# Two 64 x 64 inverses at the start of an RWKV-7 kernel, taken from VectorE and DRAM to powers on TensorE

## The chip, the cores and the metric

The kernel runs on one core of one Trainium2 chip. The metric is the device time of one execution in microseconds. Before the change it is 537.99 us, the median of three runs (537.51 to 538.75).

## What is computed

The reference has two parts. The first is a recurrence over 768 tokens, for 4 batches and 8 heads of 40 elements each:

```python
for t in range(S):
    y[:, :, t] = einsum('bhd,bhde->bhe', r_t, state)
    Sa = einsum('bhde,bhe->bhd', state, a_t)
    state = state * w_t[:, :, None, :] - einsum('bhd,bhe->bhde', Sa, b_t) + einsum('bhd,bhe->bhde', v_t, k_t)
```

The second takes y as 3072 rows of 320 numbers and applies `h = x @ w_in` (320 x 1024), `solu = h * softmax(h)`, a layer norm with the gain `g_ln`, and `@ w_out` (1024 x 320). The weights come as 64-bit floating point numbers and are turned into fp32 on the chip.

## The kernel before, in words

**Chunks.** The recurrence is computed by chunks of 64 tokens (C = 64). A chunk i holds two batches p and all eight heads, so there are N = 24 chunks: chunks 0 and 1 are the first 64 tokens of all four batches, chunks 2 and 3 the next 64, and so on. Inside a chunk the tokens depend on each other through a strictly triangular 64 x 64 matrix per batch and head (16 of them in a chunk), made from the scaled keys b and a; what is needed is the inverse of the identity minus that matrix, which `solved` applies to the right-hand sides x0.

**How an inverse is made.** `norm(i)` multiplies bT and aT of chunk i on TensorE (16 products of 64 x 64), keeps the negative in `nt` and writes its two 32 x 32 diagonal blocks to DRAM (`nt_dram`). `invert(n)` serves two chunks (2n and 2n+1, GRP = 2): it reads the blocks back so that each of 64 blocks lies in a partition of its own (`blk`), and VectorE solves for the inverse column by column in some 30 steps of two to four small instructions (lines 508, 516 and 519). The result goes to DRAM (`uu_dram`). `bring(i)` loads it for chunk i into `tu` and `uh`, `flip(i)` transposes blocks on VectorE, and `couple(i)` and `close(i)` add the off-diagonal block by two sets of 16 products on TensorE with two ScalarE copies.

**How the weights come in.** Thirteen parts of weights (five of w_in with 512 columns, eight of w_out with 320) are loaded by `land(n, queue)` and turned into fp32 by `split`: `begin_narrow` ("b", two VectorE instructions), `scale_narrow` ("s", three ScalarE instructions), `end_narrow` ("f", three VectorE instructions, and for some parts the next load on GpSimd's queue).

**Order.** All engines run in the order in which the code issues. A prologue prepares chunks 0 to 3 (`decay`, `decay_turned`, `front`, `front_b`, `norm`), then a loop runs over i from -1 to 26. Pass i solves chunk i, prepares chunk i + 5, and multiplies chunk i - 2 by w_in (`hidden`) and chunk i - 3 by w_out (`output`). The dictionary `plans` puts VectorE's work on the weights and the inverses into each pass: in "b s 5" the letters are the steps of a split and a number is so many steps of the next inverse ("o1": only of an inverse that is already due). `vector(plan)` issues one such string.

**PSUM.** Each of the tags A, B, C and h is a pair of banks for one use at a time; `pair(tag, name)` takes it, and its next user waits until it has been copied out.

In the listing, `turned` makes eight transposes for one operand, `tokens` takes an SBUF tile of [128, 2, 4, 64], `half(p)` is one half of the partitions, `in_turn` orders products so that neighbours use different quarters of the array, and `mm` (line 285) is one product.

Of the kernel before, what the change touches and what calls it, by code (L numbers as in the profile page):

```python
# [33 lines left out]
def shape_constants():  # L34
    s, t = np.arange(P)[:, None], np.arange(P)[None, :]
    same = s // C == t // C
    row = np.arange(P)[:, None] % C
    parts = dict(
        ident=np.eye(P),
        cum=same & (s <= t),  # L40
        tri=row < np.arange(C)[None, :],
        eye_hi=row == Q + np.arange(Q)[None, :],
        hi=(row >= Q).astype(np.float64),
        mean=np.full((P, P), 2.0 ** -10),
    )
    at, where = 0, {}
    for name, x in parts.items():
        where[name] = (at, at + x.shape[1])
        at += x.shape[1]
    return np.concatenate([np.asarray(x, np.float64) for x in parts.values()], 1).astype(np.float32), where  # L50
# [3 lines left out]
def kernel(  # L54
# [90 lines left out]
    def pair(tag, name):  # L145
        return psum.tile([P, 2, 512], FP32, tag=tag, name=name)
# [85 lines left out]
    def vector(plan):  # L232

        for word in plan.split():
            if word in "bsf":
                dict(b=begin_narrow, s=scale_narrow, f=end_narrow)[word]()
            else:
                some(int(word.strip("o")), (i + 2) // GRP if "o" in word else N)
# [75 lines left out]
    def ok(i):  # L314
        return 0 <= i < N


    def load_keys(i, names, queue=nc.sync):
        if not ok(i):
            return  # L320
        for n, ap in (("w", w), ("b", b), ("a", a), ("k", k)):
            if n in names:
                x = a_t[i % 3] if n == "a" else two.tile([P, H, D], FP32, tag="raw_" + n, name="raw_" + n,
                                                             bufs=2 if n == "w" else 3)
                st[i]["raw_" + n] = x
                load(x, ap, i, queue)
# [59 lines left out]
    def scaled(i, names="bk"):  # L386
        if not ok(i):
            return
        d = st[i]
        kb = d["kb"] = kb_t[i % (AHEAD + 2)]  # L390
        for n in names:
            j = H * (n == "b")
            nc.gpsimd.tensor_tensor(out=kb[:, j:j + H, 0:D], in0=d["raw_" + n], in1=heads(d["inv"]), op=ALU.mult)  # L393
# [27 lines left out]
    def front(i, t=None, y=0):  # L421
        if not ok(i):
            return lambda: None
        d = st[i]
        t = turned(pair("C", "pa") if t is None else t, y, d["raw_a"])
        aT = d["aT"] = tokens("aT", AHEAD)
        return lambda: nc.vector.tensor_tensor(out=aT[0:W2], in0=t, in1=d["ex"][0:W2, :, :, 0:C], op=ALU.mult)
# [31 lines left out]
    def shared_pair(i):  # L459

        if i not in shared:
            shared[i] = pair(turn["Y"], "py")
        return shared[i]

    def norm(i):
        if not ok(i):
            return
        d = st[i]
        t = shared_pair(i - AHEAD + 1)
        for u in in_turn(lambda p, q, g, h: (h, p ^ h)):  # L470
            p, q, g, h = u
            at = 4 * Q + (2 * q + g) * C
            mm(t[half(p ^ h), p, at:at + C], keyed(d["bT"], u), keyed(d["aT"], u))
        nt = d["nt"] = tokens("nt", AHEAD)
        nc.scalar.mul(out=nt, in_=t[:, :, 4 * Q:4 * Q + 256].rearrange("p b (j c) -> p b j c", j=4), mul=-1.0)  # L475
        n, at = divmod(i, GRP)
        if at == 0:
            blocks[n] = dram.tile([2, 2 * GRP * H, Q, Q], FP32, tag="nt_dram", name="nt_dram")
        for x in range(2):
            for e in range(2):  # L480
                home = C * x + Q * e
                queue = nc.sync if 1 < i < 4 or i == 1 and x else nc.gpsimd
                queue.dma_start(out=blocks[n][e].rearrange("(a x h) s c -> a x s h c", a=GRP, x=2)[at, x],  # L483
                                  in_=nt[home:home + Q].rearrange("p h j c -> p (h j) c")[:, :, Q * e:Q * e + Q])

    def spread(n):
        nb = two.tile([P, Q, Q], FP32, tag="blk", name="blk")
# [37 lines left out]


    def bring(i):
        if not ok(i):  # L530
            return
        d = st[i]
        d["tu"], d["uh"] = tu_t[i % 2], uh_t[i % 2]
        n, at = divmod(i, GRP)
        src = inverse[n].rearrange("c (e a x h) t -> e a c x h t", e=2, a=GRP, x=2)
        for x in range(2):
            queue = nc.sync if i or not x else nc.gpsimd
            queue.dma_start(out=d["tu"][C * x:C * x + Q, :, Q:2 * Q], in_=src[0, at, :, x])
        for x in range(2):
            nc.sync.dma_start(out=d["uh"][C * x + Q:C * x + C], in_=src[1, at].rearrange("c x h t -> c (x h) t"))  # L540

    def flip(i):
        if not ok(i):
            return
        tu = st[i]["tu"]
        nc.vector.transpose(out=tu[:, :, 0:Q], in_=tu[:, :, Q:2 * Q])

    def couple(i):
        if not ok(i):
            return lambda: None  # L550
        d = st[i]
        t = shared_pair(i)
        for u in in_turn(lambda p, q, g, h: (p ^ h, p)):
            p, q, g, h = u
            j = 2 * q + g
            x = half(p ^ h)
            mm(t[half(p), h, j * Q:j * Q + Q], d["nt"][x, p, j], d["tu"][x, 4 * p + j, 0:Q])
        return lambda: nc.scalar.activation(out=wy[:, :, :, 0:Q], in_=t[:, :, 0:4 * Q].rearrange("p h (j c) -> p h j c", j=4),  # L558
                             func=AF.Copy, scale=c_("hi"))

    def close(i):
        if not ok(i):
            return
        d = st[i]
        t = shared_pair(i)
        for u in in_turn(lambda p, q, g, h: (p, p ^ h)):
            p, q, g, h = u
            j = 2 * q + g
            mm(t[half(p ^ h), p, 384 + j * Q:384 + j * Q + Q], wy[half(p), h, j], d["uh"][half(p), H * (p ^ h) + 4 * p + j])
        nc.scalar.copy(out=d["tu"].rearrange("p (h j) c -> p h j c", h=2)[:, :, :, 2 * Q:],  # L570
                       in_=t[:, :, 384:].rearrange("p h (j c) -> p h j c", j=4))
# [307 lines left out]
    def begin_inverse(n):  # L879
        steps.append((n, invert(n)))  # L880
        next(steps[-1][1])
# [5 lines left out]
        load_keys(i, "a")  # L887
    nc.scalar.dma_start(out=g_rows, in_=moe_g_ln.rearrange("(c p) -> c p", p=P))
    load_keys(2, "w")
    for n in range(2):  # L890
        land(n, nc.sync)
    load_keys(2, "ba")
    decay(0)()
    logged(1)
    decay_turned(0)()
    plans = {
        -6: ("", "", "", "", ""),
        -5: ("b", "", "b", "", "s f"),
        -4: ("", "s", "f", "6", "2"),
        -3: ("", "", "", "", "14"),  # L900
        -2: ("", "10"),
        -1: ("b o1 s 3", "f 5", "8", "", "", "b 4"),
        0: ("", "s", "3 b", "s 2 f", "2 b 1 s", "f"),
        1: ("f b 5", "s", "8 b f", "", "s b f o1 2", "o1 3"),
        2: ("b s 5", "f s b s", "f b 5 s f 1", "b 1", "s", "f"),
        3: ("1 f", "", "11", "1 o2", "", "1"),
        4: ("4", "", "12", "", "", ""),
        5: ("7", "", "7", "2", "1", "o1"),
        24: ("o2 2", "", "", "o9", "o4", "", ""),
        25: ("1", "2", "2", "8", "1", "", ""),  # L910
    }
    for i in range(4):
        if i in (0, 3):
            scaled(i, "b")
        if i == 3:
            scaled(0, "k")
        plan = plans[i - 6]
        front(i)()
        vector(plan[0])
        front_b(i)()  # L920
        vector(plan[1])
        decay(i + 1)()
        if i == 0:
            logged(2)
            scaled(1, "b")
        vector(plan[2])
        norm(i)
        decay_turned(i + 1)()
        if i == 1:
            load_keys(3, "w")  # L930
            scaled(2, "b")
        vector(plan[3])
        if i == 1:
            begin_inverse(0)
        vector(plan[4])
        if i == 1:
            load_keys(3, "ba")
            load_keys(0, "k")
            load_keys(4, "w")
            load_values(0)  # L940
            load_r(0)
            load_keys(1, "k")
        if i == 2:
            load_keys(5, "w")
        if i == 3:
            land(2, nc.sync)
    plan = plans[-2]
    vector(plan[0])
    load_keys(2, "k", nc.gpsimd)
    load_keys(3, "k", nc.gpsimd)  # L950
    load_keys(4, "ba", nc.gpsimd)
# [6 lines left out]
    scaled(3, "k")  # L958
    load_keys(5, "ba", nc.gpsimd)
    load_keys(6, "w")  # L960
    vector(plan[1])
    decay(5)()
    load_values(1)
    load_r(1)
    scaled(4, "k")
    bring(0)
    bring(1)
    land(3, nc.sync)
    load_keys(5, "k")
    load_keys(7, "w")  # L970

# [1 line left out]
    for i in range(-1, N + LAG + 1):  # L973
# [12 lines left out]
            load_r(i + 2)  # L986
        if i == -1:
            load_values(2)
            land(4, nc.sync)
            land(len(lands), nc.sync)  # L990

        if i < EARLY - AHEAD:
# [176 lines left out]
```

## Time and profile before

| | |
|---|---|
| median of 3 runs | 537.99 us |
| span of the profiled execution | 536.5 us, the median lies 1.5 us above it |
| TensorE matmul busy | 480.7 us (90%) |
| TensorE weight load busy | 391.0 us (73%) |
| VectorE busy | 430.6 us (80%) |
| ScalarE busy | 314.1 us (59%) |
| GpSimd busy | 227.0 us (42%) |
| chain that ended last | PE 73%, DVE 17%, DMA 5%, issue 2%, ACT 2% |
| mean granted TensorE clock | 0.984 |

The shares are means over the whole span. The first quarter of the span and the rest have different limits, so they are read by stretches. PE is TensorE's matmul, PEld its weight load, DVE VectorE, ACT ScalarE, POOL GpSimd, SP the queue of SyncE that issues most DMAs. An instruction on fp32 operands shows as two records on TensorE, so 16 products are "x32". The number after L is the line in the kernel.

### The profile page before, as it was taken

What the parts mean: (1) busy time and instruction counts of PE and PEld (TensorE: products, weight loads), DVE (VectorE), ACT (ScalarE), POOL (GpSimd) and SP (SyncE); (2) the same over time, 40 slices, a digit from 0 to 9 for tenths busy, and PEclk for the clock granted to TensorE, in tenths of its full rate; (3) what the DMA queues carried; (4) which work ended last, traced back from release to release, by engine and by line L of the source; (5) the groups of instructions that cost most, each with busy time, mean ns of one, the idle gap of its engine ahead of it and who ended that gap; (6) DMA issues with size and microseconds to landing.
All of it is one profiled execution on the core that took longest, in us unless ns stands there. A gap on an engine that the chain in (4) does not pass through costs nothing.

```text
span 536.5 us, 28053 instructions
## 1 busy us (share of the span) xinstructions
PE 480.7 (90%) x12029; PEld 391.0 (73%) x12029; DVE 430.6 (80%) x1752; ACT 314.1 (59%) x627; POOL 227.0 (42%) x376
## 2 busy tenths in 40 slices
PE   4633775798989999999999999999999999999997
PEld 3522665665878878877887887788778877887766
DVE  4599987999997987997998979979989888544322
ACT  3633466488457566556666665666656555654433
POOL 4577538245253344545445263544445331210300
PEclk9999978799999999999999999999999999999999
DMA  8898889765465566674774776675554551421210
GB/s 149 153 157 160 177 142 206 165 134 124 90 131 120 102 125 138 123 151 96 147 156 104 132 150 121 118 155 109 114 118 102 108 111 43 106 65 29 61 53 24
DMA packets 194475, 63.95 MB, mean 119 GB/s; under 512 B 166840, under 2 KB 186528, under 8 KB 194352
## 3 DMA queue, kind: packets, MB, share of 16 engines
q1 hardware_dynamic: 181232, 41.60, 41.8%
q0 software_dynamic: 10768, 19.95, 15.2%
q8 instruction: 94, 1.54, 1.2%
q10 hardware_dynamic: 2352, 0.62, 0.7%
q14 instruction: 29, 0.24, 0.2%
HBM read 47.96 MB, written 14.16 MB: 116 GB/s over the span
## 4 chain that ended last, share of the span: by engine, by line
PE 73%; DVE 17%; DMA 5%; issue 2%; ACT 2%; SPq 0%; POOL 0%; ACTq 0%; POOLq 0%; DVEq 0%
PE po L285 20%; PE h L285 18%; PE px L285 6%; PE pyo L285 5%; PE py L285 5%; DVE prod L516 4%; PE ps L285 4%; DVE uu L519 3%; PE pu L285 3%; PE plnT L804 2%; PE pb L400 2%; PE pa L400 2%; PE psr L285 2%; PE pkv L400 2%; DMA uu_dram<-uu 1%
## 5 line engine op out<-in xcount | busy, mean ns | idle before, releaser
L285 PE MATMUL h<-w_in,xT 64*64 64x512 f32 (+1 forms) x1064 | 121.7, 551 | 0.7 <-issue 0.7
L285 PE MATMUL po<-w,lnT 128*128 128x160 f32 x768 | 115.2, 304 | 0.0
L516 DVE TENSOR_TENSOR prod<-blk,uu 128x48 f32<-128x48 f32 (+19 forms) x576 | 108.1, 227 | 1.3
L285 PEld LDWEIGHTS po<-w,lnT 128*128 128x128 f32 x768 | 105.5, 190 | 4.7 <-issue 0.8
L519 DVE TENSOR_TENSOR uu<-uu,prod 128x48 f32<-128x48 f32 (+19 forms) x576 | 103.8, 219 | 0.0
L483 POOL DMA_DIRECT2D nt_dram<-nt x86 | 50.8, 597 | 84.5 <-ACT nt L475 76.4
L792 POOL TENSOR_TENSOR rs<-var,mhalf 128x1 f32<-128x1 f32 x24 | 17.6, 734 | 138.2 <-ACT var L791 138.1
L761 DVE TENSOR_REDUCE nmax<-h 128x1 f32<-128x1024 f32 x24 | 29.3, 1219 | 32.9 <-PE h L285 32.9
L285 PEld LDWEIGHTS h<-w_in,xT 64*64 64x64 f32 x1064 | 36.7, 133 | 20.4 <-issue 16.7
L790 ACT ACTIVATE sq<-e,mu 128x1024 f32<-128x1024 f32 x24 | 26.9, 1119 | 24.4 <-DVE e L777 24.4
L444 DVE TENSOR_TENSOR lu<-pu,cst 128x512 f32<-128x512 f32 x24 | 16.5, 686 | 26.6 <-PE pu L285 24.8
L769 ACT ACTIVATE e<-h,nmax 128x1024 f32<-128x1024 f32 x24 | 26.7, 1111 | 17.7 <-DVE nmax L761 17.7
L558 ACT ACTIVATE wy<-py,cst 128x256 f32<-128x256 f32 x24 | 11.4, 474 | 39.2 <-PE py L285 37.1
L311 POOL DMA_DIRECT2D raw_r<-in_r_dram x48 | 33.3, 698 | 0.0
L777 DVE SCALAR_TENSOR_TENSOR e<-h,e 128x1024 f32<-128x1024 f32 x24 | 29.2, 1217 | 4.3 <-ACT e L769 4.1
L508 DVE SCALAR_TENSOR_TENSOR uu<-blk,uu 128x30 f32<-128x30 f32 (+3 forms) x144 | 30.2, 262 | 1.7 <-DMA blk<-nt_dram 0.8
L393 POOL TENSOR_TENSOR kb<-raw_b,inv 128x320 f32<-128x320 f32 x24 | 21.4, 894 | 21.1 <-DMA raw_b<-in_b_dram 13.7
L285 PE MATMUL pcum<-lw,cst 128*128 128x160 f32 x48 | 15.1, 461 | 16.7 <-ACT lw L351 16.7
L285 PEld LDWEIGHTS py<-tu,nt 64*64 64x64 f32 x768 | 17.3, 142 | 16.3 <-issue 10.7
L617 ACT COPY st<-psr 128x416 f32<-128x416 f32 (+1 forms) x44 | 14.2, 374 | 24.5 <-PE psr L285 24.4
L664 ACT ACTIVATE x<-px 128x832 f32<-128x832 f32 x24 | 20.7, 864 | 11.0 <-PE px L285 11.0
L710 DVE TENSOR_TENSOR tot<-pyo,st 104x416 f32<-104x416 f32 x44 | 23.8, 581 | 2.9 <-PE pyo L285 2.9
(154 smaller groups left out, 1095.3 us busy)
## 6 DMA issues: line engine op xcount, KB each, us to landing
xT<-x_dram SPq DMA_DIRECT2D x48, 160.0 KB, 4.2
blk<-nt_dram POOLq DMA_DIRECT2D x22, 256.0 KB, 4.7
raw_w<-in_w_dram SPq DMA_DIRECT2D x48, 80.0 KB, 3.3
raw_r<-in_r_dram POOLq DMA_DIRECT2D x48, 80.0 KB, 4.0
lv<-in_v_dram SPq DMA_DIRECT2D x48, 80.0 KB, 3.7
out_dram<-osb SPq DMA_DIRECT2D x46, 80.0 KB, 2.5
a<-in_a_dram SPq DMA_DIRECT2D x44, 80.0 KB, 4.0
raw_k<-in_k_dram SPq DMA_DIRECT2D x42, 80.0 KB, 3.8
```

Source lines behind the costliest of these rows:

```text
L285: nc.tensor.matmul(o, lhsT=lhsT, rhs=rhs, start=start, stop=stop, skip_group_check=True)
L311: queue.dma_start(out=x[half(p), :, 0:D], in_=ap[2 * bp + p, :, ci * C:(ci + 1) * C, :].rearrange("h t d -> t h d"))
L400: nc.tensor.transpose(out=t[0:W2, p, at + C * j:at + C * j + C], in_=x[half(p), 2 * j:2 * j + 2].rearrange("p a b -> p (a b)")[:, skip:ski ...
L483: queue.dma_start(out=blocks[n][e].rearrange("(a x h) s c -> a x s h c", a=GRP, x=2)[at, x], in_=nt[home:home + Q].rearrange("p h j c -> p ...
L508: nc.vector.scalar_tensor_tensor(out=u[:, c, j + 1:Q], in0=nb[:, j, j + 1:Q], scalar=u[:, c, j:j + 1], in1=u[:, c, j + 1:Q], op0=ALU.mult, ...
L516: nc.vector.tensor_tensor(out=ts[-1], in0=nb[:, j:j + 1, j + 1:Q].to_broadcast([P, hi - lo, m]), in1=u[:, lo:hi, j:j + 1].to_broadcast([P, ...
L519: nc.vector.tensor_tensor(out=u[:, lo:hi, j + 1:Q], in0=u[:, lo:hi, j + 1:Q], in1=x, op=ALU.add)
L710: nc.vector.tensor_tensor(out=by_b(tot)[:, :, :, part], in0=y[:, :, :, part], in1=by_b(state_of(i)[:, x])[:, :, :, 0:HW], op=ALU.add)
L761: nc.vector.tensor_reduce(out=nmax, in_=d["h"], axis=AX.X, op=ALU.max, negate=True)
L769: nc.scalar.activation(out=e, in_=d["h"], func=AF.Exp, bias=d["nmax"], accum_out=d["esum"])
L777: nc.vector.scalar_tensor_tensor(out=d["e"], in0=d["h"], scalar=1.0 / DFF, in1=d["e"], op0=ALU.mult, op1=ALU.mult, accum_out=d["mu"])
L790: nc.scalar.activation(out=pair("A" if i == N - 2 else "h", "sq").rearrange("p a b -> p (a b)"), in_=d["e"], func=AF.Square, scale=-float( ...
```

## The change

For chunks 0 and 1 the inverse is no longer made by `invert`, DRAM, `flip`, `couple` and `close`. `norm_powers(i)` makes the triangular matrix R and its transpose with two sets of 16 products, masks them on VectorE, and puts an identity beside R. Then six calls of `hop(i, k)` square and multiply: R and the sum lie side by side in `rx`, the transpose in `rt`, and the last call copies the sum into `tu`. The hops of the two chunks alternate, with the preparation of chunks 2 and 3 and four parts of the weights' split between them. `bring`, `flip`, `couple` and `close` return at once for i < GRP. Loads of weights stand at other places on SP's queue, and the plans of passes -1 to 2 are new. The core of the diff:

```diff
+        up=-1.0 * (row < np.arange(C)[None, :]),
+        low=-1.0 * (row > np.arange(C)[None, :]),
...
-    def norm(i):
+    def norm(i, t=None):
...
-        t = shared_pair(i - AHEAD + 1)
+        t = shared_pair(i - AHEAD + 1) if t is None else t
...
+    def norm_powers(i):
+        d = st[i]
+        t = pair("C", "pn")
+        flat = two.tile([P, 2, 8, C], FP32, tag="kvT", name="powers", bufs=1) if i == 0 else \
+            two.tile([P, Q, Q], FP32, tag="blk", name="powers")
+        flat = flat.rearrange("p a b c -> p (a b c)" if i == 0 else "p a b -> p (a b)")
+        d["rx"] = flat.rearrange("p (q u e) -> p q u e", q=2, u=4)
+        d["rt"] = tokens(("psi", "rT")[i])
+        for x in range(2):
+            nc.vector.tensor_copy(out=d["rx"][half(x)].rearrange("p q u e -> p (q u) e")[:, :, C:],
+                                  in_=ident[half(x), half(x)].unsqueeze(1).to_broadcast([C, 8, C]))
+        for y, (one, other) in enumerate((("bT", "aT"), ("aT", "bT"))):
+            for u in in_turn(lambda p, q, g, h: (h, p ^ h)):
+                p, q, g, h = u
+                at = 256 * y + (2 * q + g) * C
+                mm(t[half(p ^ h), p, at:at + C], keyed(d[one], u), keyed(d[other], u))
+        for y, (dst, mask) in enumerate(((d["rx"][:, :, :, 0:C], "up"), (d["rt"], "low"))):
+            for p in range(2):
+                nc.vector.tensor_tensor(
+                    out=dst[:, :, 2 * p:2 * p + 2], op=ALU.mult,
+                    in0=t[:, p, 256 * y:256 * y + 256].rearrange("p (q g c) -> p q g c", q=2, g=2),
+                    in1=c_(mask).unsqueeze(1).unsqueeze(1).to_broadcast([P, 2, 2, C]))
+
+    turned_powers = []
+
+    def hop(i, k):
+        d = st[i]
+        if not turned_powers:
+            turned_powers.append(pair("A", "pr"))
+        tr = turned_powers[0][:, :, 256 * i:256 * i + 256].rearrange("p q (u c) -> p q u c", u=4)
+        t = pair("BC"[i], "px").rearrange("p q (u e) -> p q u e", u=4)
+        rx, rt, opened = d["rx"], d["rt"], set()
+        last, lo = k == 5, C * (k >= 4)
+        turns = [((p ^ h ^ (q & k & 1)), p ^ h ^ (q & (k + 1) & 1), q, 2 * p + g)
+                 for p, q, g, h in in_turn(lambda p, q, g, h: (p ^ h ^ (q & k & 1), q))]
+        if not last:
+            for x, y, q, u in turns:
+                mm(tr[half(y), q, u], rx[half(x), q, u, 0:C], rt[half(x), q, u])
+            nc.vector.tensor_copy(out=rt, in_=tr)
+        for x, y, q, u in turns:
+            mm(t[half(y), q, u, lo:], rt[half(x), q, u], rx[half(x), q, u, lo:], start=(y, q) not in opened, stop=False)
+            opened.add((y, q))
+            mm(t[half(y), q, u, C:], ident[half(x), half(x)], rx[half(x), q, u, C:], start=False)
+        if not last:
+            nc.scalar.copy(out=rx[:, :, :, lo:], in_=t[:, :, :, lo:])
+        else:
+            d["tu"] = tu_t[i % 2]
+            tu = d["tu"].rearrange("x (p q g) c -> x q p g c", p=2, q=2)
+            for q in range(2):
+                nc.scalar.copy(out=tu[:, q, :, :, Q:], in_=t[:, q, :, C:].rearrange("x (p g) c -> x p g c", p=2))
...
     load_keys(2, "w")
+    load_keys(2, "ba")
     for n in range(2):
         land(n, nc.sync)
-    load_keys(2, "ba")
...
-        -6: ("", "", "", "", ""),
-        -5: ("b", "", "b", "", "s f"),
-        -4: ("", "s", "f", "6", "2"),
-        -3: ("", "", "", "", "14"),
-        -2: ("", "10"),
-        -1: ("b o1 s 3", "f 5", "8", "", "", "b 4"),
-        0: ("", "s", "3 b", "s 2 f", "2 b 1 s", "f"),
-        1: ("f b 5", "s", "8 b f", "", "s b f o1 2", "o1 3"),
-        2: ("b s 5", "f s b s", "f b 5 s f 1", "b 1", "s", "f"),
-        3: ("1 f", "", "11", "1 o2", "", "1"),
+        -1: ("", "b s 2", "f 8", "6", "", "b 4"),
+        0: ("s f b", "s 3", "4 f", "b", "3 s", "f"),
+        1: ("b s 5", "f", "8 b s", "f b", "s 2", "f"),
+        2: ("b s 4", "f 2", "8 b s", "f", "", "2"),
+        3: ("1", "", "11", "1 o2", "", "1"),
...
+    scaled(0, "b")
+    front(0)()
+    front_b(0)()
+    decay(1)()
+    logged(2)
+    scaled(1, "b")
+    norm_powers(0)
+    decay_turned(1)()
+    front(1)()
+    front_b(1)()
+    decay(2)()
+    norm_powers(1)
+    decay_turned(2)()
+    load_keys(3, "w")
+    scaled(2, "b")
+    load_keys(3, "ba")
+    load_keys(0, "k")
+    load_values(0)
+    load_r(0)
+    land(2, nc.sync)
+    load_keys(4, "w")
+    load_keys(1, "k")
+    land(3, nc.sync)
+
+    for n in range(6):
+        hop(0, n)
+        if n in (0, 2):
+            i = 2 + n // 2
+            if i == 3:
+                scaled(3, "b")
+                scaled(0, "k")
+            t = pair("h", "pa")
+            outs = front(i, t, 0), front_b(i, t, 1)
+            for evict in outs:
+                evict()
+        if n in (1, 3):
+            decay(3 + n // 2)()
+        if n > 0:
+            vector(("b", "s f b", "s f b", "s f b", "s f")[n - 1])
+        hop(1, n)
+        if n in (1, 3):
+            i = 2 + n // 2
+            norm(i, pair("h", "py"))
+            decay_turned(i + 1, pair("h", "pei"))()
+            if i == 2:
+                load_keys(5, "w")
...
-    vector(plan[1])
     decay(5)()
...
-    bring(0)
-    bring(1)
-    land(3, nc.sync)
+    land(4, nc.sync)
```

## What was predicted

> **What bounds the kernel now.** I read the page's 40 slices first, then engine time by stretches, the chain of waits, the groups, and last the timeline of the first 130 us.
>
> ```profile
> PE   4633775798989999999999999999999999999997
> DVE  4599987999997987997998979979989888544322
> ACT  3633466488457566556666665666656555654433
> ```
>
> A slice is 13.4 us. From the twelfth on TensorE is nearly full, one chunk every 18.5 us. Before, it idles and VectorE is full. The change lies wholly in that start, so the question is when the loop gets going. VectorE's first instruction of each pass is the product into aT (line 427): 49.17 us (pass -1), 67.13 (0), 83.28 (1), 106.28 (2), 127.27 (3), 148.59 (4). I cut the stretches there.
>
> ```profile
> 27.40:49.17 21.77, 8.91 (x112) 7.15 (x112) 21.41 (x113) 5.81 (x13) 17.06 (x26) 1.00 0.92 160
> 49.17:67.13 17.96, 9.72 (x235) 8.83 (x237) 17.89 (x86) 8.77 (x19) 10.13 (x15) 1.00 0.86 170
> 67.13:83.28 16.15, 11.21 (x342) 9.80 (x338) 13.86 (x53) 11.98 (x23) 6.81 (x11) 0.79 0.81 149
> 83.28:106.28 23.00, 16.82 (x442) 14.34 (x436) 20.00 (x87) 11.75 (x25) 10.91 (x18) 0.78 0.83 185
> 163.00:181.60 18.60, 18.07 (x506) 15.21 (x509) 16.23 (x61) 12.17 (x27) 8.37 (x13) 1.00 0.45 100
> ```
>
> The columns are the stretch, its length, then busy time of PE, PEld, DVE, ACT, POOL. VectorE works 21.41 of 21.77 us and 17.89 of 17.96; the last row is the steady loop, bound by TensorE. So passes -1 to 3 cost what VectorE has to do, and whatever delays pass -1 delays the end.
>
> ```profile
> 21.64 5.66 DMA blk<-nt_dram
> 27.98 2.26 DVE uu L508 x10
> ...
> 49.17 0.68 DVE aT L427
> ...
> 81.91 7.82 DMA uu_dram<-uu
> 89.78 0.33 SPq L538
> 90.21 3.77 DMA tu<-uu_dram
> 94.06 0.45 DVE tu L546
> ```
>
> The chain shows the trip through DRAM before inverse 0 (blk) and, for inverse 1, the one after it. Only the first goes; inverse 1 still serves chunks 2 and 3 and keeps its trips.
>
> ```profile
> L516 DVE TENSOR_TENSOR prod<-blk,uu 128x48 f32<-128x48 f32 (+19 forms) x576 | 108.1, 227 | 1.3
> L519 DVE TENSOR_TENSOR uu<-uu,prod 128x48 f32<-128x48 f32 (+19 forms) x576 | 103.8, 219 | 0.0
> L508 DVE SCALAR_TENSOR_TENSOR uu<-blk,uu 128x26 f32<-128x26 f32 (+5 forms) x36 | 9.0, 305 | 1.0 <-DMA blk<-nt_dram 0.8
> ```
>
> The first two are whole-run groups, the third is that of 27.4 to 106.3 us. With the whole run's 30.2 us of L508, twelve inverses cost 242.1 us of VectorE, 20.2 each.
>
> **What goes.** 20.2 us of VectorE, flips of chunks 0 and 1 (2 x 0.43), their couple and close on TensorE, ScalarE copies of 0.37 to 0.6 us, and DRAM trips of which only the wait for blk (until 27.4) stood in the way. All of it falls between 25.8 and 49.2 us or beside VectorE's work. Moving the loads for chunk 2 ahead of land(0), land(1) on SP costs nothing: these weights are now first read at about 33 us. land(2) to land(4) stand earlier behind key loads and are read from 70 us on.
>
> **What comes: prices.**
>
> ```profile
> 62.20 1.65 PE L285 MATMUL px<-lv,psi 64*64 64x104 f32 x32
> 119.00 0.94 PE L285 MATMUL px<-lv,psi 64*64 64x104 f32 x32
> 84.48 1.03 ACT L583 COPY kvT<-pkv 104x1024 f32<-104x1024 f32 x1
> L440 DVE COPY bT<-pa 104x512 f32<-104x512 f32 x14 | 9.5, 678 | 0.0
> ```
>
> The same 16 products took 1.65 us at 62 us and 0.94 at 119. Until 66.9 us every form runs at the slow pace, though the page prints a clock of 1.00 there: no clock record lies before that time, so the durations decide. Less a tail of 0.27, 16 products of 104 columns stream in 1.38 us, 0.83 ns per column and product. In a hop, the squaring (16 products of 64) is then 0.86, the second set (16 of 128 and 16 of 64) 2.56, and 1.71 in hops 4 and 5, which leave R out. I count 0.25 for a tail and 0.06 per hand-over (pei began 0.05 after ei ended). Copying the transpose (VectorE) is 0.68, copying R and the sum (ScalarE) 1.03, half of it 0.6. Masks: four of 256 elements at 0.4 (0.69 is the price of 512); identities two at 0.45 (wy, 256, took 0.23).
>
> The order of issue decides, since each queue runs in it. The second set reads the transpose that VectorE has just rewritten, so it waits for that copy. From round 2 the weight split (s: three ScalarE steps, 2.05; f: three VectorE steps, 2.05, starting 1.46 after s; b: two, 0.85) stands between the hops: s queues behind the copy of R that waits for hop 0, f waits for s, and hop 1's transpose copy queues behind f and b. TensorE has nothing else.
>
> Start: the 32 products of norm_powers(0) from 11.94 us end at 14.1, masks 15.8, the turned a of chunk 1 (same PSUM) lets aT(1) end at 17.1, pcum(2) to 18.3, 32 products to 20.4, masks to 22.0. Rounds, from hop 0's transpose copy to the next:
> - 0: copy 0.74, second set 2.56, two turns for chunk 2 1.05, squaring 1.17, copy 0.74, second set 2.56, squaring 1.17 = 9.99.
> - 1: copy 0.74, set 2.87, R 1.03, log 0.53, pcum 1.38, squaring 1.17, copy 0.74, set 2.87, R 1.03, nt 0.66, pei 0.6, squaring 1.17 = 14.79.
> - 2: copy and set 3.61, R 1.03, bT 0.58, s 1.46, f 2.05, b 0.85, copy 0.74, set 2.56, squaring 1.17 = 14.05.
> - 3: 3.61, R 1.03, log 0.53, pcum 1.44, two exponentials 0.87, s, f, b 4.36, copy and set 3.61, R 1.03, nt 0.66, pei 0.6, squaring 1.17 = 18.91.
> - 4: copy 0.74, set 2.02, R 0.6, s, f, b 4.36, copy 0.74, set 1.71 = 10.17.
> - 5 and the way to the loop: set 2.02, tu 0.8, s 2.05, tu 0.8, v and r 0.92, log 0.53, pcum 1.38, turn 0.66 = 9.16.
>
> 22.0 + 77.1 = 99.1 us for the aT that came at 49.17: **+49.9**.
>
> The loop: two weight splits fewer (2 x 2.9), one flip in each of passes -1 and 0 fewer (0.86), two steps of the inverse more (1.9): -4.8. In pass -1 only two steps stand before the first masks, so VectorE waits for turns, kvT and scores, some 3 us; pass 0's "s f b" waits too, but VectorE idled 2.3 us there anyway. Net -2, between -5 and +3. The profiled span is 536.5, the median 537.99: 1.5 lie around it and stay. 538.0 + 49.9 - 2 = **586**.
>
> Unknowns: the clock in the hops, and products that follow each other on the same quarter of the array. Elsewhere quarters rotate product by product (four start within some 30 ns); here the second product of a unit sits right behind the first. If they still overlap, 2.56 holds; if a unit must end first, it doubles. I take 2.56: at 283.02 us pu's products started past earlier ones queued for another quarter.
>
> **Rivals.**
> - TensorE at full pace in the hops. TensorE's terms, 41.9 us of the rounds and some 5 of the start, halve, which takes 23 us: the loop begins at 76, and 538.0 + 26.8 - 2 = 563. For: round 0 has 4.5 us of products without a gap. Against: from 10.6 to 17.9 us TensorE was busy with gaps of 0.1 and py at 16.2 still took 1.13 (0.65 at 70.3), and rounds 2 to 4 leave it idle for 6 us at a time; at 73.7 us a thinner stretch took the pace away. The Trainium skill, "TensorE: Matmul & The Clock Gate", Part 1, has the clock at half by default and released by about 3.4 us of sustained activity; by that rule the clock opens in round 0, which the stretch from 10.6 speaks against.
> - Same-quarter products don't overlap: eight sets of the chain grow by 2.56 us and three by 1.71, 26 in all: 612. Against: pu at 283.02. Partly so, some 600.
> - Faster: VectorE's sum alone decides. 20.2 + 0.86 go, ten copies (6.8) and masks with identities (2 x 2.5) come: -9.3, 529. It needs the hops to run beside VectorE's work, from a loop start before 49 us on. For it speaks that VectorE is the full engine. Against: the next inverse is begun only behind the hops, and the chain at full pace still ends at 76.
> - The change doesn't do what it says: "without VectorE's steps" is half true, ten copies stand in the chain. If the second sets didn't wait for them, ten terms of 0.99 would go (copy 0.74 and tail 0.25), 576, inside the forecast's own range; the order of the code speaks against it.
>
> **Numbers.** Forecast 0.66 (its own range 574 to 597: loop -5 to +3, a few sets at full pace, VectorE held by POOL's kb products as at 64.1 us, where a 0.42 us step took 1.09). Full pace 0.18, no overlap 0.12, faster 0.03, an unmeasurable change 0.01 (a measurement can tell 0.2%, 1.1 us). Range 560 to 602: it takes in full pace and partial overlap.
>
> **What would show it.** Right: the first aT of the loop near 99 us; TensorE at about six tenths and VectorE at four in slices 4 to 6; second sets of about 2.8 us; hop 1's transpose copy right behind L197 in rounds 2 to 4; afterwards passes of 16 to 23 us and the same 18.5. Wrong: aT near 76 with sets of 1.4; sets over 5 us; or a loop that starts before 60.

## The result and the profile after

The changed kernel takes 605.2 us (median of four runs, 603.93 to 606.95) against 537.91 (537.51 to 538.75): ratio 1.126, 95% interval 1.123 to 1.129. It is slower by 67 us, 19 us more than the 586 forecast and 3 us above the upper end of the range. The profiled execution took 606.95 us, with a span of 605.2 (before 536.5).

The 40 slices of the page, now 15.1 us each:

```profile
PE   4865452657679897999999999999999999999997
DVE  5313231898786968978979989798897989833422
ACT  3232442364547445566666666656666655564443
POOL 4110009745334152446355353553635532121110
```

VectorE is down to one to three tenths in slices 3 to 6, GpSimd to nothing in slices 4 to 6, and TensorE, which now does the work, has four to six tenths there. In these slices no engine is full. GpSimd's 9 and 7 in slices 7 and 8 are what it could not do before.

The places where the product into aT starts on VectorE, read from the timelines of both kernels (line 427 before, 429 after), give the account:

| | first aT | pass -1 | 0 | 1 | 2 | 3 | 4 | 5 | from pass 6 to the end |
|---|---|---|---|---|---|---|---|---|---|
| before | 49.17 | 18.0 | 16.1 | 23.0 | 21.0 | 21.3 | 19.6 | 18.4 | 349.9 |
| after | 100.18 | 22.9 | 15.2 | 25.1 | 24.2 | 23.6 | 24.1 | 18.8 | 351.0 |

The start costs 51.0 us more, passes -1 to 5 cost 16.5, the rest 1.1: together 68.7, the difference of the spans. The engine times by stretches (columns as before: the stretch, its length, PE, PEld, DVE, ACT, POOL, clock, DMA share, GB/s):

```profile
22.00:77.00 55.00, 33.13 (x962) 30.45 (x966) 13.38 (x23) 17.42 (x26) 1.67 (x2) 0.80 0.23 45
77.00:100.18 23.18, 8.31 (x254) 7.21 (x246) 5.25 (x9) 8.62 (x18) 9.49 (x15) 0.72 0.44 102
100.18:123.08 22.90, 11.54 (x237) 10.16 (x237) 18.22 (x81) 10.23 (x22) 16.44 (x23) 0.57 0.95 163
138.32:163.45 25.13, 17.78 (x436) 16.14 (x434) 18.96 (x75) 13.27 (x27) 9.48 (x15) 0.63 0.64 131
211.27:235.34 24.07, 19.45 (x496) 16.48 (x490) 16.71 (x75) 10.79 (x21) 8.74 (x15) 0.93 0.57 118
```

In the rounds (a round is one hop of each of the two chunks; first row) GpSimd works 1.67 of 55 us and the DMA engines 23%. In pass -1 (third row) both are crowded: GpSimd 16.44 of 22.90 and the DMA 95%. In passes 1 and 4 (last two rows) VectorE works 18.96 of 25.13 and 16.71 of 24.07; before, it worked 20.00 of 23.00 and 16.68 of 19.63 us in these two, so about the same work, and some 3 us of idle time where there are now 6 and 7. So three things beside the rounds themselves cost time, and each has its line. First the groups of the whole run (line, engine, tiles, count, busy time, mean ns of one, idle time before them and what ended it):

```profile
L536 ACT COPY powers<-px 128x1024 f32<-128x1024 f32 (+1 forms) x10 | 9.3, 927 | 39.1 <-PE px L287 39.1
L287 PE MATMUL px<-powers,rT 64*64 64x128 f32 (+1 forms) x192 | 13.2, 355 | 17.6 <-DVE rT L530 16.6
L187 POOL DMA_DIRECT2D bits<-in_moe_w_out_dram x7 | 4.2, 595 | 64.8 <-DMA w<-in_moe_w_in_dram 42.4
```

The second row is the chain that the prediction described: TensorE waits 16.6 us for chunk 1's transpose copy. The third row was in no step of it. These are weight loads on GpSimd's queue that a split's `f` issues (`land`, line 187); each takes a buffer that an earlier part leaves, and so waits for that part's split, which stands between the rounds. (The first row below names a DMA as what ended the wait. That split's last VectorE step, L212, ended at 81.13, 0.29 us before, just as it ended 0.30 before the second load; in the run with the copy behind the second set, below, the same row names L212.) GpSimd's timeline and two lines of the timelines of TensorE and VectorE, in order of time (start, length, engine, line, idle time before it and its releaser):

```profile
81.42 0.62 POOL L187 DMA_DIRECT2D bits<-in_moe_w_out_dram  x1 [42.36 <-DMA w<-in_moe_w_in_dram]
90.35 0.55 POOL L187 DMA_DIRECT2D bits<-in_moe_w_out_dram  x1 [8.30 <-DVE w_in L212]
...
94.97 1.36 POOL L313 DMA_DIRECT2D a<-in_a_dram  x2
...
97.66 0.34 PE L402 MATMUL pb<-cst,a 64*104 64x64 f32 x1 [6.66 <-DMA a<-in_a_dram]
...
100.18 0.69 DVE L429 TENSOR_TENSOR aT<-pb,ex 104x512 f32<-104x512 f32 x1 [10.13 <-ACT rT L412]
```

GpSimd stands for 42.36 us at one load, then 8.30 at the next; the key loads queued behind (before, they ran at 31 to 36 us) leave only from 90.89 on, a of chunk 4 arrives for TensorE at 97.66, and the first aT of the loop starts after 10.13 us in which VectorE has nothing to do. The last copy into tu had ended at 89.05.

The two other lines, from the timelines of ScalarE in pass 1 and VectorE in pass 4:

```profile
153.30 0.56 ACT L201 ACTIVATE scale<-scale,top 128x320 int32<-128x320 int32 x1 [5.08 <-DVE scale L198]
...
154.91 0.45 ACT L613 ACTIVATE wy<-py,cst 128x256 f32<-128x256 f32 x1
```

```profile
228.95 0.68 DVE L557 TENSOR_TENSOR uu<-blk,above 64x512 f32<-64x512 f32 x1 [6.54 <-DMA blk<-nt_dram]
```

In pass 1 the entry "8 b s" of the plan makes ScalarE wait 5.08 us for a `b` that stands behind eight inverse steps on VectorE, and `couple`'s copy wy, on the way to the solve, waits behind it. In pass 4 VectorE waits 6.54 us for the blocks of an inverse that it begins a pass too early.

### The profile page after: what moved, and what is told of

The parts are those of the page before. It is cut to its first block, busy times and chain, and to the rows that moved or that the text cites. A ratio compares the mean times of both kernels' runs of the same rounds, so it can differ in the third digit from the quotient of the medians.

```text
span 605.2 us, 29993 instructions
## 1 busy us (share of the span) xinstructions
PE 518.1 (86%) x13053; PEld 429.2 (71%) x13053; DVE 424.7 (70%) x1662; ACT 322.7 (53%) x635; POOL 221.6 (37%) x367
## 3 DMA queue, kind: packets, MB, share of 16 engines
q8 instruction: 102, 1.67, 1.2%
## 4 chain that ended last, share of the span: by engine, by line
PE 70%; DVE 13%; DMA 5%; ACT 5%; issue 3%; POOL 2%; SPq 1%; ACTq 0%; POOLq 0%; DVEq 0%
PE po L287 17%; PE h L287 15%; PE px L287 9%; PE pyo L287 5%; PE py L287 4%; PE ps L287 3%; PE pu L287 3%; DVE prod L571 3%; DVE uu L574 2%; PE plnT L859 2%; PE pa L402 2%; PE pb L402 2%; DMA uu_dram<-uu 1%; PE psr L287 1%; PE pkv L402 1%
## 5 line engine op out<-in xcount | busy, mean ns | idle before, releaser
L574 DVE TENSOR_TENSOR uu<-uu,prod 128x60 f32<-128x60 f32 (+12 forms) x528 | 97.6, 225 | 0.0
L571 DVE TENSOR_TENSOR prod<-blk,uu 128x60 f32<-128x60 f32 (+12 forms) x528 | 95.5, 221 | 1.3
L485 POOL DMA_DIRECT2D nt_dram<-nt x80 | 47.0, 594 | 88.0 <-ACT nt L477 87.0
L287 PEld LDWEIGHTS h<-w_in,xT 64*64 64x64 f32 x1064 | 37.5, 134 | 18.8 <-issue 15.4
L446 DVE TENSOR_TENSOR lu<-pu,cst 128x512 f32<-128x512 f32 x24 | 16.5, 687 | 29.7 <-PE pu L287 27.9
L536 ACT COPY powers<-px 128x1024 f32<-128x1024 f32 (+1 forms) x10 | 9.3, 927 | 39.1 <-PE px L287 39.1
L287 PE MATMUL px<-powers,rT 64*64 64x128 f32 (+1 forms) x192 | 13.2, 355 | 17.6 <-DVE rT L530 16.6
L187 POOL DMA_DIRECT2D bits<-in_moe_w_out_dram x7 | 4.2, 595 | 64.8 <-DMA w<-in_moe_w_in_dram 42.4
L287 PE MATMUL pcum<-lw,cst 128*128 128x160 f32 x48 | 13.5, 420 | 16.1 <-ACT lw L353 16.1
L287 PE MATMUL pu<-x,tu 64*64 64x104 f32 x768 | 26.0, 262 | 1.5 <-ACT ex L421 1.5
```

The lines of the kernel that those rows point to most:

```text
L287: nc.tensor.matmul(o, lhsT=lhsT, rhs=rhs, start=start, stop=stop, skip_group_check=True)
L571: nc.vector.tensor_tensor(out=ts[-1], in0=nb[:, j:j + 1, j + 1:Q].to_broadcast([P, hi - lo, m]), in1=u[:, lo:hi, j:j + 1].to_broadcast([P, ...
L574: nc.vector.tensor_tensor(out=u[:, lo:hi, j + 1:Q], in0=u[:, lo:hi, j + 1:Q], in1=x, op=ALU.add)
```

## The experiments

Each kernel is the changed one with the edit shown, unless said otherwise; "..." stands for lines left out. Ratios are to the kernel before, timed beside each run (536.5 to 537.0 us). Lines of kernels with an insertion are up to five higher.

### The key loads in front of the waiting weight load

```diff
+        if n == 2:
+            load_keys(2, "k", nc.gpsimd)
+            load_keys(3, "k", nc.gpsimd)
+            load_keys(4, "ba", nc.gpsimd)
         if n in (1, 3):
             decay(3 + n // 2)()
...
-    load_keys(2, "k", nc.gpsimd)
-    load_keys(3, "k", nc.gpsimd)
-    load_keys(4, "ba", nc.gpsimd)
```

> Issues the key loads of chunks 2, 3 and 4 on GpSimd's queue in round 2, ahead of the two weight loads that wait there for the f of rounds 4 and 5. Theory Q (the late loop start and part of the long pass -1 come from GpSimd's queue: the weight load of round 4 stood in it from 39 to 81 us, that of round 5 until 90.4, and the keys of chunk 4 behind it landed at 97.6): VectorE's first aT of the loop comes at 91 to 93 us instead of 100.2, pass -1 shortens from 22.9 to 19 to 21 us, the time falls from 605 to 592 to 597. Rival H (the hops themselves set the start, the queue only fills a wait that is there anyway): aT stays within 2 us of 100, 603 to 606.

597.51 us (592.38 to 599.62), ratio 1.111 (1.106 to 1.117). The first aT comes at 92.42, inside the expected 91 to 93, with the last tu copy at 88.68, nearly as in the changed kernel: of the 11.1 us between the two there, 7.4 were GpSimd's queue. But pass -1 takes 24.3 us, not 19 to 21. VectorE's waits in it and GpSimd's timeline say why:

```profile
DVE uu L557 <- DMA blk<-nt_dram: 4.3, 1, 4.3
```

```profile
94.69 1.06 POOL L547 DMA_DIRECT2D blk<-nt_dram  x2 [0.42 <-issue]
```

The blocks' read for inverse 1 stood behind the second waiting load and left at 94.69, in the middle of everything that had piled up. Part of the delay was moved, not removed.

### All of GpSimd's queue in front of the weight loads

The two loads that `f` issues in the rounds are kept back until keys, blocks and scalings have been issued:

```diff
+    held = [None]
...
-            land(LANDS_NEXT[load], nc.gpsimd)
+            if held[0] is None:
+                land(LANDS_NEXT[load], nc.gpsimd)
+            else:
+                held[0].append(LANDS_NEXT[load])
...
+    held[0] = []
     for n in range(6):
...
     load_keys(5, "ba", nc.gpsimd)
+    for n in held[0]:
+        land(n, nc.gpsimd)
+    held[0] = None
```

> The two weight loads that f of rounds 4 and 5 issues on GpSimd's queue are held back until the key loads, the blocks of inverse 1 and the key scaling stand in the queue. Theory Q, whole: GpSimd and the transfers work during the hops, so that besides the start (aT at 91 to 93) the wait for blk (2.4 us) and the key scaling beside VectorE leave pass -1, which falls from 22.9 to 18 to 19.5 us: 591 to 594. Rival: pass -1 is long for TensorE and ScalarE work at its start (turns, kvT, scores) and stays at 22 us or more: 596 to 598, as with the keys alone moved.

592.01 us (591.2 to 593.69), ratio 1.103 (1.101 to 1.105). First aT at 92.55, and pass -1 takes 17.3 us, less than the 18.0 before:

```profile
76.27 1.06 POOL L552 DMA_DIRECT2D blk<-nt_dram  x2 [28.91 <-DMA raw_w<-in_w_dram]
...
84.18 0.60 POOL L187 DMA_DIRECT2D bits<-in_moe_w_out_dram  x1
90.59 0.57 POOL L187 DMA_DIRECT2D bits<-in_moe_w_out_dram  x1 [5.82 <-DVE w_in L212]
```

The blocks' read leaves 24 us earlier (100.22 in the changed kernel) and behind the weight load that still waits stand no longer the keys and the blocks, but later loads (raw_r, at 91.15). 13 us of the change's 67 were this one queue: 7.6 ahead of the loop and 5.6 in pass -1.

### The split's ScalarE steps ahead of the inverse's steps

```diff
-        1: ("b s 5", "f", "8 b s", "f b", "s 2", "f"),
-        2: ("b s 4", "f 2", "8 b s", "f", "", "2"),
+        1: ("b s 5", "f", "b s 8", "f b", "s 2", "f"),
+        2: ("b s 4", "f 2", "b s 8", "f", "", "2"),
```

> In the plans of passes 1 and 2 'b s' stands ahead of the eight steps of the inverse, not behind them; nothing else. Theory A (the new plans put three ScalarE steps s, which wait for VectorE's b behind eight steps, ahead of the copy into wy on ScalarE's queue; TensorE's second set of couple and close, all of the pass, waits 4.4 us for it): wy in pass 1 comes some 3.5 us earlier, pass 1 falls from 25.1 to 21 to 22.5 us, pass 2 from 24.2 by 1 to 3 us, the time to 599 to 601.5. Rival C (TensorE at half pace makes these passes long): pass 1 keeps over 24 us, 603 to 606.

595.75 us (591.78 to 597.34), ratio 1.108 (1.104 to 1.113); passes 1 to 3 take 21.6, 21.5, 21.5 instead of 25.1, 24.2, 23.6. The gain of 9.5 is larger than the 4 to 6 expected: passes 1 to 3 all shorten, not only the one with the wait of 5 us. In pass 1 the mean clock stayed (0.63, now 0.64), in pass 2 it rose from 0.86 to 1.00; what of that pass's gain is the clock was not separated.

### Two steps of the inverse too many

```diff
-        2: ("b s 4", "f 2", "8 b s", "f", "", "2"),
+        2: ("b s 4", "f 2", "8 b s", "f", "", "1"),
```

> One step of the inverse fewer in the plan of pass 2, so that inverse 3 ends exactly with the plan of pass 4 and inverse 4 isn't begun there. Theory T (inverse 4's first step stands in VectorE's queue for its blocks from DRAM, 6.5 us of idle in pass 4): that wait goes, pass 4 falls from 24.1 to about 19.5 us, the time to 600 to 602. Rival C (passes 1 to 4 are long because TensorE runs at half pace there, and VectorE's wait only lies beside that): pass 4 keeps 23 us or more, 604 to 606.

603.65 us (603.18 to 605.0), ratio 1.125 (1.122 to 1.127): a gain of 1.5 us, less than the 3 to 5 expected, and VectorE still waits 5.2 us for blk in pass 4. The cause was right, the count was not: by the time the plan's last "2" is reached, the due inverse has already been finished, and both of its steps go to the next one. With both taken away:

```diff
-        2: ("b s 4", "f 2", "8 b s", "f", "", "2"),
+        2: ("b s 4", "f 2", "8 b s", "f", "", ""),
```

> Both steps at the end of pass 2 are taken out. The run with one step fewer still had the wait for blk (5.2 us) in pass 4: the due inverse is finished ahead of the last entry of the plan, so that the entry's two steps both went to inverse 3 and the count was two too high. Theory T: now the wait for blk in pass 4 goes, pass 4 takes 19 to 20.5 us instead of 24.1, passes 2 and 3 gain 1 to 2 us as in that run, and the time falls to 598 to 601. Rival C: pass 4 stays over 22.5 us because something else ends late there, 602 to 604.

597.08 us (596.05 to 602.33), ratio 1.114 (1.109 to 1.119). The wait is gone, and passes 2 to 4 take 22.7, 21.5, 19.2 instead of 24.2, 23.6, 24.1.

### The weight split's place between the hops

```diff
+        if n > 1:
+            vector("s")
         hop(0, n)
...
-        if n > 0:
-            vector(("b", "s f b", "s f b", "s f b", "s f")[n - 1])
...
         hop(1, n)
...
+        if n > 0:
+            vector(("b", "f b", "f b", "f b", "f")[n - 1])
```

> Same work, other order: ScalarE's s is issued ahead of hop 0, VectorE's f and b behind hop 1's transpose copy. Theory O (the order of issue puts s, f and b, 4.4 us, into the chain of rounds 2 to 4 and 2 us of s into round 5): the hops end 13 to 15 us earlier (last copy into tu at 74 to 76 instead of 89.0), the weight loads on GpSimd's queue too, and the time falls to 589 to 593. Rival P (TensorE's products bound the rounds): the hops end less than 4 us earlier, 601 to 605.

587.83 us (587.19 to 588.27), ratio 1.094 (1.091 to 1.097). The last tu copy ends at 72.13, 17 us earlier, a little better than expected. The prediction's chain (s behind the copy of R, f behind s, chunk 1's transpose copy behind f) is what rounds 2 to 4 hang on.

### The transpose copy behind the second set

`tensor_copy(out=rt)` is moved behind the second set, so that the set multiplies with the power as it stood before this round's squaring; it no longer waits for VectorE. The edit also changes what is computed, as the code shows (no run measures it). With the copy behind, the six rounds multiply the sum by identity plus R, R², R⁴ and so on, which is the inverse. With the copy ahead, as in the changed kernel, the first factor is already identity plus R², so tu leaves out the factor with R itself; and for the heads with q = 1 the set reads the square that belongs to the other h, since the copy has put it in that half.

```diff
-            nc.vector.tensor_copy(out=rt, in_=tr)
         for x, y, q, u in turns:
...
         if not last:
+            nc.vector.tensor_copy(out=rt, in_=tr)
             nc.scalar.copy(out=rx[:, :, :, lo:], in_=t[:, :, :, lo:])
```

> VectorE's copy of the transpose is issued behind the second set of products, which then reads the transpose of the round before and waits for no copy in its own round. Theory O: ten waits of about 1 us go, and in rounds 2 to 4 hop 1's second set no longer stands behind f and b, which then only delay the next round's squaring: the hops end 12 to 17 us earlier, 588 to 594. Rival S (the chain of s, f, b and the copies on ScalarE and VectorE bounds the rounds also without that wait): 6 to 10 us earlier, 595 to 600.

581.5 us (580.87 to 582.52), ratio 1.083 (1.080 to 1.086): the largest single step, 24 us where 11 to 17 were expected. The last tu copy ends at 67.17, 22 us earlier. The stretch from the first squaring to the last tu copy, in the changed kernel and in this one:

```profile
20.77:89.05 68.28, 39.89 (x1210) 36.56 (x1208) 18.65 (x34) 24.09 (x40) 3.17 (x5) 0.80 0.28 56
20.59:67.17 46.58, 32.30 (x1210) 29.97 (x1208) 19.08 (x35) 24.20 (x40) 3.18 (x5) 0.89 0.36 76
```

For the same products TensorE is busy 7.6 us less, and the records show full pace from 23.7 to 44.2 and 54.4 to 68.1 us, against seven stretches of 3.4 to 10.2 us between 27.2 and 92.1 in the changed kernel. The other 14 us are waiting that went: the prediction counted ten terms of 0.99 for these copies, and chunk 1's second sets no longer stand behind s, f and b either. How the 14 us divide between these two was not separated.

### All five edits

GpSimd's queue in front of the weight loads, the split's steps ahead of the inverse's, both surplus steps taken away, the split's place between the hops, and the copy behind the second set.

> All repairs together: split steps around the hops, copy behind the second set, weight loads last, s ahead of the steps, no overshoot. If the causes add (14 to 17 us of order, 5 more from the copy, 8 and 4 from the queue, of which the part under the hops shrinks with them, 4 from wy, 4 from the overshoot): first aT at 56 to 62 us, passes -1 to 4 in 112 to 120 us as before, 541 to 553. Rival: order and copy overlap (they free the same wait), the first aT stays at 65 or later, 555 to 565.

555.8 us (554.99 to 559.18), ratio 1.037 (1.034 to 1.041), the lower end of the rival. The single gains add up to 72 us, together they are 49: the copy's and the split's place shorten the same rounds. Windows of this kernel's rounds:

```profile
22.00:64.00 42.00, 28.28 (x1171) 25.89 (x1163) 18.66 (x30) 21.85 (x34) 15.38 (x22) 1.00 0.53 107
```

The clock is full from 23.2 to 64.1 us, and TensorE works 28.28 of 42.00 (after: 33.13 of 55, for less of the same rounds). First aT at 69.79; passes -1 to 5 together take 132.9 us, against 137.5 before: **the loop is 4.6 us shorter**, close to the -4.8 of work that the prediction took out of it. VectorE's busy time in these passes fell by less, 3.2 us (127.72 to 124.53), so that closeness is in part chance. So all that is left of the loss is the start, 20.6 us.

### What the start costs without five of the six rounds

From the kernel of all five edits:

```diff
-        hop(0, n)
+        if n == 5:
+            hop(0, n)
...
-        hop(1, n)
+        if n == 5:
+            hop(1, n)
```

> The kernel of all five edits (555.8 us, first aT of the loop at 69.8), with rounds 0 to 4 of the powers left out for both chunks, so that tu holds only what the last round makes of N; the weight splits, turns and decays between the rounds stay. It asks what the start costs without the rounds. Theory: the rounds stand in series with what lies between them, and each of the five costs 4 to 5 us of the start; the last tu copy ends by 45 us, the first aT comes at 46 to 50, as before, and the total is 531 to 538 (the loop is 2 to 5 us shorter than that of the kernel before). Rival: the splits, decays and turns with their own hand-overs would hold the loop back without the rounds; the first aT comes at 56 or later and the total is 541 or more.

543.37 us (540.79 to 544.74), ratio 1.013 (1.009 to 1.018), so still slower, by less than 2%. Here tu holds no more than identity plus R, so the run measures time and makes no inverse. The total is in the rival's range (541 or more), not the theory's; the first aT, at 52.94, lies between the two (46 to 50, and 56). So the five rounds cost 16.9 us of the start, 3.4 each, less than expected; and **with one round left the loop still starts 3.8 us later than before**, with VectorE's 20 us of inverse 0 gone as well. The two runs differ in the clock too: before the loop its records show full pace from 23.2 to 64.1 us with the rounds, and from 44.9 to 48.3 alone without them. VectorE's and ScalarE's timelines of this kernel:

```profile
30.05 0.69 DVE L434 TENSOR_TENSOR aT<-pa,ex 104x512 f32<-104x512 f32 x1 [7.11 <-ACT scale L201]
...
43.21 0.69 DVE L210 SCALAR_TENSOR_TENSOR bits<-bits,scale 128x512 int32<-128x512 int32 x1 [5.04 <-ACT scale L202]
```

```profile
24.84 0.44 ACT L370 ACTIVATE ei<-pcum 128x320 f32<-128x320 f32 x1 [1.58 <-PE pcum L292]
...
26.85 0.60 ACT L482 ACTIVATE nt<-py 128x512 f32<-128x512 f32 x1 [1.25 <-PE py L292]
28.21 0.59 ACT L426 COPY ex<-pei 104x512 f32<-104x512 f32 x1 [0.76 <-PE pei L407]
28.70 0.73 ACT L201 ACTIVATE scale<-scale,top 128x512 int32<-128x512 int32 x1
```

The decay, the norm and the turns of chunks 2 to 5 run as one serial chain over ScalarE and TensorE, with the splits in between in ScalarE's order; VectorE waits for it. In this order the chain, with the splits and the one round in it, reaches to 52.94. What the preparation would take alone isn't shown: the round that is left may be most of the 3.8 us, if it costs what the other five cost on average. In the kernel before, that preparation stood beside VectorE's inverse 0.

### The weight splits behind the rounds

From the kernel of all five edits:

```diff
-        if n > 1:
-            vector("s")
...
-        if n > 0:
-            vector(("b", "f b", "f b", "f b", "f")[n - 1])
...
+    for word in ("b", "s f b", "s f b", "s f b", "s f"):
+        vector(word)
```

> The kernel of all five edits, with the ten weight-split steps (s, f, b) taken out from between the rounds and put behind round 5. It asks how much of the splits lies beside TensorE's rounds there. Theory: with the copy behind the second set and the split moved, most of the splits (some 16 us of VectorE and ScalarE steps, four s of 2.05, four f of 2.05 partly beside them, four b of 0.85) lie beside the rounds; the last tu copy ends 6 to 12 us earlier than 65.5, the first aT comes 4 to 10 us later than 69.8, and the total is 560 to 567. Rival: splits and rounds still stand in series; tu ends at 52 or earlier, the first aT stays within 2 us of 69.8 and the total is within 3 us of 555.8.

565.44 us (563.9 to 566.71), ratio 1.055 (1.052 to 1.057), the theory's total. The last tu copy ends at 62.20, only 3.3 us earlier than with the splits between (6 to 12 were expected), and the first aT at 80.05, 10.3 later. Once s and f are placed well, the splits cost the rounds 3.3 us. What remains from the first squaring (20.63) to the last tu copy, 41.6 us, is the rounds and the preparation of chunks 2 and 3 between them; TensorE is busy 29.84 us of it and waits for the rest.

## Why the prediction was wrong, point by point

**What bounds the kernel.** "Whatever delays pass -1 delays the end" held: from pass 6 on the two kernels differ by 1.1 us. That passes -1 to 3 "cost what VectorE has to do" was read from VectorE's full stretches, and it was incomplete: the run without five rounds shows a second chain that, with one round in it, ends 3.8 us later than VectorE's did, so taking inverse 0 off VectorE did not bring the loop forward even with five of six rounds left out. That speaks against the rival "faster" (529) in this order of issue.

**The start**, 99.1 predicted, 100.18 measured, is right only because two errors cancel. The transpose copies of hop 0 start at 21.97, 30.68, 43.72, 58.20 and 74.21 us:

| | predicted | measured |
|---|---|---|
| first copy | 22.0 | 21.97 |
| round 0 | 9.99 | 8.71 |
| round 1 | 14.79 | 13.04 |
| round 2 | 14.05 | 14.48 |
| round 3 | 18.91 | 16.01 |
| round 4 and 5 to the end of tu | 15.84 | 14.84 |
| from tu to the first aT | 3.49 | 11.13 |

The rounds are 6.5 us shorter than worked out, mainly because a part of them ran at the full clock, which opened at 27.23, in round 0. Two lines of the chain, the second set of round 0, of chunk 0 before the clock opens and of chunk 1 after it:

```profile
22.80 2.97 PE px L287 x56
...
28.45 1.60 PE px L287 x51
```

2.97 is the sum's 2.56 with tail and hand-over (2.87 there), 1.60 is near half of it. So the rival of full pace came true in part, for at most 6.5 of its 23 us; the stretch from 10.6 us, which the prediction held against it, lies in windows of 1280, 1304 and 896 weighted columns, all below the bound of the last section. The rival of no overlap on the same quarter of the array was false: its sets would have taken over 5 us. The last row is the GpSimd queue. "The order of issue decides, since each queue runs in it", says the prediction, and it looked at SP's queue, whose loads it called free, but not at GpSimd's: `f` issues a weight load there, and the key loads stand behind it.

**The loop** is the step that failed: "Net -2, between -5 and +3", measured +16.5, which is 18.5 of the 19 us between the forecast and the result. The work in it was counted about right (-4.8; the kernel of all five edits shows -4.6, and 3.2 less of VectorE's busy time). What was left out is order:
- pass -1: "waits for turns, kvT and scores, some 3 us". It was GpSimd's queue and the crowding behind it; undone, the pass goes from 22.9 to 17.3.
- passes 1 to 3: the new plans were read for VectorE's work, not for ScalarE's queue. "8 b s" puts wy behind a split that waits for VectorE; undone, 72.9 us become 64.6.
- passes 2 to 4: "two steps of the inverse more (1.9)" priced the steps as work. They are two steps beyond a finished inverse, and begin the next one before its blocks are there; undone, 71.9 us become 63.4.

The last two overlap in passes 2 and 3, and the clock rose with both there, so their gains can't be added. None of the three is work; each is a place in an order.

**Copies.** "If the second sets didn't wait for them, ten terms of 0.99 would go (576)": the direction was right and the size less than half of the 24 us measured. Left out were the clock, which opens for longer, and that the second sets of chunk 1 then no longer stand behind the split either. The change is described as making the inverse in another way; with the copy where the changed kernel has it, its rounds leave out a factor, as said above.

**The signs named** held for aT (99 against 100.18, by the luck told above), for the transpose copy of hop 1 right behind the split (L199 ends at 53.70, the copy starts at 53.62), for the second sets of 2.8 us in the slow stretches (2.9 to 3.0), and for the pass of 18.5; in slices 4 to 6 VectorE had two and three tenths instead of four and TensorE four and five instead of six, and the passes in between went to 25 us instead of 23.

What stays open: none of the kernels run beats the one before. The 20.6 us of start left in the kernel of all five edits are 16.9 for five rounds and 3.8 for what the run without them still holds: the serial preparation, the splits and one round. Whether another order of that would bring it under 49 us wasn't tried.

## What to carry to other kernels

When a step is moved or a plan rewritten, walk each queue it touches, GpSimd's and ScalarE's too: an instruction that waits for a buffer costs nothing itself, and here 13 us through what stood behind it. An engine that is full in a stretch is not proof that emptying it helps; look for the second chain, and work out where it ends without the first. In a chain of small products with copies on other engines between them, the waiting is a large part of the time: from the first squaring to the last tu copy TensorE worked 39.9 of 68.3 us in the changed kernel, and 29.8 of 45.1 in the kernel of all five edits.

## What the runs showed of the hardware that was not expected

In these traces the clock is not granted for being busy. Two windows of the changed kernel's start, both before the first clock record (so the page's 1.00 says nothing):

```profile
16.99:20.40 3.41, 3.41 (x72) 2.96 (x74) 1.17 (x4) 1.35 (x3) 1.14 (x2) 1.00 1.12 192
23.81:27.23 3.42, 3.42 (x83) 3.17 (x80) 0.32 (x1) 1.01 (x1) 0.00 (x0) 1.00 0.62 109
```

TensorE is busy throughout in both. After the first and the one between, the second set still takes 2.97 us (at 22.80), after the second 1.60 (at 28.45), and the first record of full pace stands at 27.23. They differ in how much of the array the products use: counting the columns of each product, weighted by its share of the 128 x 128 array (a 64 x 64 product counts a quarter, a 40 x 64 product, as in norm_powers, 0.16), the first window has 1224 and the second 1616; the one between them, 74% busy, has 1256. Records change only on a grid of 3.413 us, so the first 260 us of all twelve profiles were cut at that grid. A bound of 1350 weighted columns in a window tells the pace of the next one in 897 of 915 windows, in both directions, and in 195 of the 198 in which the pace changes; the best bound on the busy share alone gets 758, on unweighted columns 772; 17 windows over 95% busy left the slow pace in place, and 30 windows below 95% (down to 79%) ended it. The Trainium skill, "TensorE: Matmul & The Clock Gate", Part 1, has the clock released by about 3.4 us of sustained activity; the length agrees with the grid, but by these counts it is the part of the array in use that decides, not the time. The bound is inferred from counts and fitted to the windows that it is counted on; no run varied it by itself.
